# Attention of a fused attention and feed-forward kernel: a fixed table of places for its steps, V's clearing on two engines, the first q on ScalarE's queue

## Chip, cores and metric

One core of one Trainium2 chip. The metric is the device time of one execution in microseconds: 607.05 us for the kernel before, the median of three runs (606.36 to 607.29).

## What is computed

Causal attention over 2 batches, 12 heads, 448 positions and 64 columns a head, then a gated layer (768 to 1536 to 768), then a hard-swish layer (768 to 2048 to 768) on the 896 tokens.

```python
scores = scale * np.matmul(q, k.transpose(0, 1, 3, 2))
scores = np.where(mask, -1000000000.0, scores)
attn = np.exp(scores - max); attn = attn / (sum + 1e-09)
x = np.matmul(attn, v)               # heads side by side: 896 x 768
x = (sigmoid(x @ w_gate) * (x @ w_val)) @ w_out
h = x @ w_in
out = (h * np.clip(h + 3.0, 0.0, 6.0) / 6.0) @ w2_out
```

The weights arrive as 64-bit floats, as their words, and are decoded to 32 bits on the chip.

## The kernel before

Every product is made from three: each operand is split into a high part, rounded to the form that TensorE takes, and a low part, the rest (`TERMS`: high by high, high by low, low by high). Attention works on 12 pairs of heads, pair p = 0 to 11. Six pairs make one batch. After the attention the first feed-forward layer runs in units of a 128-column strip of weights against all tokens, batch 0's half and batch 1's half.

The attention is cut into steps, each a function that issues a few instructions on one engine. The names below are those of the code's keys; a number behind a pair's step is a tile of query rows (0 to 3, of 64, 128, 128 and 128 rows), a tile group of scores or a group of key chunks.

- SP (the queue for loads): **Lq**, **Lk**, **Lv** (`load`, L238 on) and **W** (`load_unit`, L98 on), the raw weights of units 0 to 2.
- TensorE (PE): **T** q and k (`t_pe`, L273), transposes; **S0** to **S2** (`s_pe`), the scores of tiles 0 and 1, of tile 2, of tile 3; **C0** to **C3** (`c_pe`), transposes of the normalised rows; **D0** to **D3** (`d_pe`), products with v; **F** (`f_pe`), the first two units' products for batch 0, 6 steps of 3 products each; **Z** (`z_pe`), idle products on a zero tile, 30 of them.
- ScalarE (ACT): **Th** (`t_hi`), high parts of q and k; **E0** to **E3** (`s_exp`), exponentials and row sums; **H0** to **H3** (`c_hi`) and **X** (`x_hi`), high parts of C and of the output; Wa and Wf of the decoding.
- VectorE (DVE): **Tl** (`t_lo`), low parts; **M0** to **M3** (`s_max`); **R0** to **R3** (`s_rcp`); **J0** to **J3** (`c_lo`); Xl; Wb to We and Wg of the decoding (shift, clamp, join, sign, low part).
- GpSimd (POOL): **V** (`v_hi`, `v_lo`, L262 on), v's two parts into the padded tiles `vpad`; **N0** to **N3** (`s_nrm`), rows times reciprocals.

`rings` says which step must have ended before a buffer is used again. Two PSUM pairs hold scores: S2 of a pair may start when E0 and E1 have read S0's, S0 of the next pair when E2 has read S1's, S1 when E3 has read S2's. One PSUM bank holds the output of D, so D0 waits for Xl of the pair before. C has two banks, so C2 waits for J0 and C3 for J1.

Every engine runs its instructions in the order in which they were issued. That order comes from `emit_in_order(rank)`: a list scheduler. It keeps a modelled clock per engine, takes of all steps whose inputs are done the one that could start first, and breaks ties by `rank`, the pair's number plus a number from the table `LATE` by the step's letter. Steps carry a modelled duration and an engine for this. Ahead of it the code clears the zero halves of `vpad` (three pairs of tiles, two halves each) on VectorE and builds the masks.

Of the kernel before, what the change touches and what calls it, by code (L numbers as in the profile page):

```python
# [31 lines left out]
def kernel(  # L32
# [12 lines left out]
    nc = tc.nc  # L45
    B, H, S, D = q.shape
# [3 lines left out]
    P = 128  # L50
# [7 lines left out]
    NP = B * NPAIR  # L58
# [152 lines left out]
    with tc.manual_schedule():  # L211

        with ExitStack() as actx:
            def pool(name, bufs, **kw):
                return actx.enter_context(tc.tile_pool(name=name, bufs=bufs, **kw))
# [6 lines left out]
            p_sm = pool("p_sm", 8)  # L222
# [203 lines left out]
            def product(cols, stationary=P):  # L426

                return max(cols / 2.4 + 3, stationary / 1.2)


            steps = []
            for p in range(NP):
                def add(key, eng, ns, after, fn, *args):
                    steps.append(((p, key), eng, ns, [(p, a) for a in after], fn, (p, *args)))

                for nm in ("q", "k", "v"):
                    add("L" + nm, "sp", 1500, [], load, nm)
                for nm in ("q", "k"):
                    add("T" + nm, "pe", 390, ["L" + nm], t_pe, nm)
                    add("Th" + nm, "act", 430, ["T" + nm], t_hi, nm)  # L440
                    add("Tl" + nm, "dve", 540, ["Th" + nm], t_lo, nm)
                add("Vh", "pool", 1040, ["Lv"], v_hi)
                add("Vl", "pool", 2150, ["Vh"], v_lo)
                for i, ts in enumerate(STILES):
                    work = sum(
                        6 * product(Q1[t], Q1[t] - Q0[t]) + 2 * product(Q1[t] - Q0[t], 0) for t in ts
                    )
                    add(f"S{i}", "pe", work, ["Tlq", "Tlk"], s_pe, ts)
                    for t in ts:
                        add(f"M{t}", "dve", 70 + 2.1 * Q1[t], [f"S{i}"], s_max, t)  # L450
                for t in range(NQ):
                    n = Q1[t]
                    add(f"E{t}", "act", 605 + 1.67 * n, [f"M{t}"], s_exp, t)
                    add(f"R{t}", "dve", 85, [f"E{t}"], s_rcp, t)
                    add(f"N{t}", "pool", 488 + 1.67 * n, [f"R{t}"], s_nrm, t)
                for g in range(NG):
                    m = WIDTH[g]
                    tiles = [f"N{t}" for t in range(NQ) if Q1[t] > GROUPS[g][0][0] * D]
                    add(f"C{g}", "pe", 0.87 * m, tiles, c_pe, g)
                    add(f"H{g}", "act", 60 + m / 1.2, [f"C{g}"], c_hi, g)  # L460
                    add(f"J{g}", "dve", 70 + m / 0.96, [f"H{g}"], c_lo, g)
                    work = sum(3 * product(S - c * D) for c, _ in GROUPS[g])
                    add(f"D{g}", "pe", work, [f"J{g}", "Vl", f"D{g - 1}"][: 2 + (g > 0)], d_pe, g)
                add("Xh", "act", 430, [f"D{NG - 1}"], x_hi)
                add("Xl", "dve", 540, ["Xh"], x_lo)

            WARM = 30
# [3 lines left out]

            for i in range(WARM):
                steps.append(((0, f"Z{i:02}"), "pe", 300, [], z_pe, (0,)))
# [3 lines left out]
            for u in range(3):  # L477
                w = f"{u}"
                def add(key, eng, ns, after, fn, *args):
                    steps.append(((NP - 3, key + w), eng, ns, after, fn, (u, *args)))  # L480
# [5 lines left out]
                add("Wa", "act", 740, own("W"), dec_scale)  # L486
                add("Wb", "dve", 470, own("W"), dec_shift)
                add("Wc", "dve", 470, own("Wa"), dec_clamp)
                add("Wd", "dve", 870, own("Wb", "Wc"), dec_join)
                add("We", "dve", 870, own("Wd"), dec_sign)  # L490
                add("Wf", "act", 740, own("We"), dec_hi)
                add("Wg", "dve", 870, own("Wf"), dec_lo)
# [6 lines left out]
            for u in range(2):  # L499
                for i in range(KD):  # L500
                    steps.append(
                        ((NP, f"F{u}{i}"), "pe", 570,
                         [(NP - 3, f"Wg{u}"), (NPAIR - 1, "Xl")] + [(NP, f"F{u}{i - 1}")] * (i > 0),
                         f_pe, (u, i))
                    )


            def every(*uses):
                return [((p, a), (p, z)) for p in range(NP) for a, z in uses]
# [9 lines left out]
                (1, [((0, "Tk"), (0, "Tlk"))] + every(("D0", "Xl"))),  # L519
# [3 lines left out]
                (2, every(*((f"S{i}", f"E{ts[-1]}") for i, ts in enumerate(STILES)))  # L523
                    + [((NP, f"F{u}0"), None) for u in range(2)]),
# [3 lines left out]
                (2, [((NP - 3, f"Wa{u}"), (NP - 3, f"Wg{u}")) for u in range(3)]),  # L528
            ]

            HOP = 200

            def emit_in_order(rank):


                left = {s[0]: s for s in steps}
                eng_of = {s[0]: s[1] for s in steps}
                need = {key: set(s[3]) for key, s in left.items()}
                for n, uses in rings:
                    for (a, _), (_, z) in zip(uses[n:], uses):  # L540
                        need[a].add(z)
                    for (a, _), (b, _) in zip(uses[1:], uses):
                        need[a].add(b)
                then = {key: [] for key in left}
                for key, n in need.items():
                    for a in n:
                        then[a].append(key)
                ready = {key: 0 for key, n in need.items() if not n}
                free, done = {}, {}
                while ready:  # L550
                    at, _, key = min(
                        (max(free.get(eng_of[key], 0), t), rank(key), key)
                        for key, t in ready.items()
                    )
                    ready.pop(key)
                    _, eng, ns, _, fn, args = left.pop(key)
                    done[key] = free[eng] = at + ns
                    if eng == "sp":
                        done[key] += 1800
                    fn(*args)  # L560
                    for k in then[key]:
                        if all(a in done for a in need[k]):
                            ready[k] = max(
                                done[a] + HOP * (eng_of[a] != eng_of[k]) for a in need[k]
                            )
                assert not left

            def rank(key):
                p, name = key
                return p + LATE[name[0]]  # L570


            LATE = {
                "J": 1.3, "C": 0.07, "R": -0.94, "E": 0.6, "T": -2.37, "H": 1.3, "S": -0.1,
                "X": 1.38, "M": -2.4, "V": 0.28, "N": 1.41, "D": 2.66, "L": 0.0, "W": 0.85,
                "F": 9.0, "Z": 99.0,
            }


# [15 lines left out]
            emit_in_order(rank)  # L595
# [674 lines left out]
```

## Time and profile before

| What | Value |
|---|---|
| median of three runs | 607.05 us |
| lowest, highest | 606.36, 607.29 us |
| profiled execution: span from first to last instruction | 604.3 us |
| profiled execution: its time beside the span | not given by the page; median less span is 2.75 us |
| TensorE busy | 591.4 us, 98% |
| VectorE, ScalarE, GpSimd busy | 476.4, 346.1, 136.7 us |
| DMA moved | 82.64 MB, mean 137 GB/s |

The attention takes about the first fifth of the span. A busy share of TensorE holds products that wait in its pipeline, so a full share in the attention does not mean that it does useful work all the time; the chain of waits and the starts in the timeline tell that apart. In the timeline an instruction's duration is longer than its distance to the next one where the two overlap, so work is counted by differences of starts.

### The profile page before, as it was taken

What the parts mean: (1) busy time and instruction counts of PE and PEld (TensorE: products, weight loads), DVE (VectorE), ACT (ScalarE), POOL (GpSimd) and SP (SyncE); (2) the same over time, 40 slices, a digit from 0 to 9 for tenths busy, and PEclk for the clock granted to TensorE, in tenths of its full rate; (3) what the DMA queues carried; (4) which work ended last, traced back from release to release, by engine and by line L of the source; (5) the groups of instructions that cost most, each with busy time, mean ns of one, the idle gap of its engine ahead of it and who ended that gap; (6) DMA issues with size and microseconds to landing.
All of it is one profiled execution on the core that took longest, in us unless ns stands there. A gap on an engine that the chain in (4) does not pass through costs nothing.

```text
span 604.3 us, 9071 instructions
## 1 busy us (share of the span) xinstructions
PE 591.4 (98%) x3372; PEld 535.8 (89%) x3372; DVE 476.4 (79%) x739; ACT 346.1 (57%) x680; POOL 136.7 (23%) x195
## 2 busy tenths in 40 slices
PE   8999999999999999999999999999999999999997
PEld 4788788899998999998999999988999899999997
DVE  6789998568797898988967787888999888867601
ACT  3898998735656656667443333387677645533200
POOL 4889988401111111110000000012222000000000
PEclk9999999999999999999999999999999999999999
DMA  7665341036985876674334434367988514437002
GB/s 167 137 178 132 81 143 33 0 79 167 263 178 133 215 183 180 166 177 129 82 114 150 154 115 135 94 165 165 235 217 200 140 53 112 131 124 227 23 1 91
DMA packets 86684, 82.64 MB, mean 137 GB/s; under 512 B 35312, under 2 KB 77040, under 8 KB 86640
## 3 DMA queue, kind: packets, MB, share of 16 engines
q1 hardware_dynamic: 80448, 64.50, 35.9%
q0 software_dynamic: 6192, 17.57, 15.8%
q8 instruction: 26, 0.43, 0.3%
q14 instruction: 18, 0.15, 0.1%
HBM read 61.73 MB, written 2.75 MB: 107 GB/s over the span
## 4 chain that ended last, share of the span: by engine, by line
PE 56%; DVE 27%; ACT 9%; POOL 3%; issue 3%; DMA 2%; SPq 0%; ACTq 0%; POOLq 0%; DVEq 0%
PE w L750 25%; PE m L1203 12%; PE m L190 10%; DVE b L128 4%; DVE b L134 4%; DVE lo L158 4%; PE pav L392 3%; ACT hi L153 3%; PE s L309 2%; DVE g L1171 2%; PE pt L365 2%; DVE b L124 2%; DVE raw L120 2%; ACT pr L337 2%; DVE g L182 2%
## 5 line engine op out<-in xcount | busy, mean ns | idle before, releaser
L1203 PE MATMUL m<-hi,g 128*128 128x384 f32 x448 | 114.0, 335 | 0.6 <-DVE g L1171 0.6
L153 ACT CAST hi<-b 128x768 fp32r<-128x768 f32 x35 | 29.0, 835 | 104.3 <-DVE b L134 100.1
L1203 PEld LDWEIGHTS m<-hi,g 128*128 128x128 f32 x448 | 80.8, 188 | 1.2 <-DVE g L1171 1.2
L1203 PE MATMUL m<-lo,g 128*128 128x384 f32 x224 | 74.9, 335 | 0.4 <-DVE lo L158 0.4
L750 PE MATMUL w<-T,hi 128*128 128x448 f32 x252 | 72.4, 368 | 1.4 <-ACT g2r L767 1.4
L190 PE MATMUL m<-g,hi 128*128 128x448 f32 x288 | 70.1, 365 | 0.0
L134 DVE SCALAR_TENSOR_TENSOR b<-raw,b 128x768 int32<-128x768 int32 x68 | 66.0, 971 | 2.3
L128 DVE SCALAR_TENSOR_TENSOR b<-b,raw 128x768 int32<-128x768 int32 x68 | 65.4, 962 | 2.3
L115 ACT ACTIVATE b<-raw 128x768 f32<-128x768 f32 x68 | 61.2, 905 | 0.0
L124 DVE TENSOR_SCALAR b<-b 128x768 f32<-128x768 f32 x68 | 38.1, 561 | 25.5 <-ACT b L115 25.2
L190 PEld LDWEIGHTS m<-g,hi 128*128 128x128 f32 x288 | 54.1, 188 | 4.3
L144 POOL DMA_DIRECT2D lo<-S x26 | 25.2, 971 | 131.0 <-ACT lo L143 102.5
L352 POOL TENSOR_SCALAR pr<-pr,rc 64x64 f32<-64x64 f32 (+3 forms) x96 | 52.6, 565 | 9.1 <-DVE rc L346 7.3
L158 DVE TENSOR_TENSOR lo<-b,hi 128x768 fp32r<-128x768 f32 x35 | 33.3, 957 | 27.0 <-ACT hi L153 26.9
L750 PEld LDWEIGHTS w<-T,hi 128*128 128x128 f32 x252 | 47.2, 188 | 6.3 <-ACT g2r L767 1.8
L190 PE MATMUL m<-x,hi 128*128 128x448 f32 x192 | 49.1, 367 | 0.0
L337 ACT ACTIVATE pr<-s,nm 64x64 f32<-64x64 f32 (+3 forms) x96 | 44.4, 469 | 5.7 <-PE s L319 5.0
L750 PE MATMUL w<-T,lo 128*128 128x448 f32 x126 | 46.5, 369 | 0.7 <-DMA lo<-S 0.5
L1203 PEld LDWEIGHTS m<-lo,g 128*128 128x128 f32 x224 | 42.0, 188 | 0.7 <-DVE lo L158 0.7
L392 PE MATMUL pav<-pth,vpad 128*128 128x448 f32 (+6 forms) x168 | 41.0, 309 | 0.0
L190 PE MATMUL m<-g,lo 128*128 128x448 f32 x144 | 40.9, 366 | 0.0
L190 PEld LDWEIGHTS m<-x,hi 128*128 128x128 f32 x192 | 35.7, 188 | 2.7
(139 smaller groups left out, 1248.8 us busy)
## 6 DMA issues: line engine op xcount, KB each, us to landing
raw<-in_moe_w_out_dram SPq DMA_DIRECT2D x28, 768.0 KB, 4.5
raw<-in_moe_w_in_dram SPq DMA_DIRECT2D x16, 768.0 KB, 4.7
lo<-S POOLq DMA_DIRECT2D x26, 384.0 KB, 4.3
raw<-in_moe_w_gate_dram SPq DMA_DIRECT2D x12, 768.0 KB, 5.2
raw<-in_moe_w_val_dram SPq DMA_DIRECT2D x12, 768.0 KB, 5.0
k<-in_k_dram SPq DMA_DIRECT2D x24, 112.0 KB, 2.7
q<-in_q_dram SPq DMA_DIRECT2D x24, 112.0 KB, 3.0
v<-in_v_dram SPq DMA_DIRECT2D x24, 112.0 KB, 2.9
```

The costliest lines, as they stand in the source:

```text
L115: nc.scalar.activation(b, words(u)[0].bitcast(F32), AF.Copy, scale=REBIAS)
L124: nc.vector.tensor_scalar(b, b, UPPER_MAX, -UPPER_MAX, op0=ALU.min, op1=ALU.max)
L128: nc.vector.scalar_tensor_tensor(bi, bi, 3, words(u)[1], op0=ALU.logical_shift_left, op1=ALU.bitwise_or)
L134: nc.vector.scalar_tensor_tensor(bi, words(u)[0], -(2 ** 31), bi, op0=ALU.bitwise_and, op1=ALU.bitwise_or)
L153: nc.scalar.copy(hi, part_t[u])
L158: nc.vector.tensor_sub(lo, part_t.pop(u), split_t[u][0].bitcast(F32))
L190: nc.tensor.matmul(ps[:, b, :S], lhsT=w[a][:, i * P : (i + 1) * P], rhs=x(c, k0 + i, b), start=(first and i == 0 and n == 0), stop=(last a ...
L337: nc.scalar.activation(pr[:, :, j], ps[:, j].rearrange("p (c d) -> p c d", d=D), AF.Exp, bias=nm[:, j : j + 1], accum_out=sm[:, j : j + 1],)
L352: nc.gpsimd.tensor_scalar(pr[:, :, j], pr[:, :, j], rc[:, j : j + 1], 1.0, op0=ALU.mult, op1=ALU.mult)
L392: nc.tensor.matmul(live["pav", p][:, c * D :], lhsT=vpad[p % NV][a][:, c], rhs=pt[e][:, off : off + S - c * D], start=(c == 0 and m == 0), ...
L750: nc.tensor.matmul(ps, lhsT=w[a][:, k * P : (k + 1) * P], rhs=x[:, c, i], start=(first and i == 0 and n == 0), stop=(i == HK - 1 and n == ...
L1203: nc.tensor.matmul(po[t], lhsT=g2[2 * s + i][a][:, t * P : (t + 1) * P], rhs=w[e][:, i * HC : (i + 1) * HC], start=(s == 0 and i == 0 and ...
```

## The change

The list scheduler, its modelled engines and durations, `rank` and `LATE` go. Instead `AT` gives each step of a pair a place, the pair adds `p * PERIOD + SHIFT[p]`, and `OWN` gives places to the idle products, the units' decoding and F. A step's place is raised until it lies behind all that it needs, and steps are issued in order of place. The numbers only sort; no instruction waits for one. The number of idle products falls from 30 to 21, the ring of score pairs now names all tiles of a group, p_sm has 16 buffers instead of 8, three of the six tiles of `vpad` are cleared by GpSimd, and pair 0's q is loaded from ScalarE's queue.

```diff
-            p_sm = pool("p_sm", 8)
+            p_sm = pool("p_sm", 16)
...
+                eng = nc.scalar if (p, nm) == (0, "q") else nc.sync
                 for j in range(2):
-                    nc.sync.dma_start(
+                    eng.dma_start(
...
+            PERIOD = 16779
+            SHIFT = [
+                -14386, -7787, -4533, -4454, -1883, 702, 2710, 4993, 6496, 8505, 11307, 14490,
+            ]
+            AT = {
+                "C0": 43560, "C1": 43561, "C2": 51916, "C3": 51917, "D0": 57245, "D1": 57246, "D2": 57247, "D3": 65288,
...
+            OWN = {
...
-            WARM = 30
...
-            for i in range(WARM):
-                steps.append(((0, f"Z{i:02}"), "pe", 300, [], z_pe, (0,)))
+            for i in range(len(WARM)):
+                steps.append(((0, f"Z{i:02}"), [], z_pe, (0,)))
...
-                add("W", "sp", 2000, [], load_unit)
+                add("W", [(2 * u + 2, "Lv")], load_unit)
...
-            def emit_in_order(rank):
+            def emit_in_order():
...
+                def when(key):
+
+                    if key not in place:
+                        p, name = key
+                        at = OWN[name] if name in OWN else p * PERIOD + SHIFT[p] + AT[name]
+                        place[key] = max([at] + [when(a) + 1 for a in need[key]])
+                    return place[key]
+
+                for key in sorted(left, key=lambda key: (when(key), key)):
+                    _, fn, args = left[key]
                     fn(*args)
...
-            for pair in vpad:
-                for t in pair:
+            for i, pair in enumerate(vpad):
+                for x, t in enumerate(pair):
+                    eng = nc.gpsimd if 2 * i + x < 3 else nc.vector
                     for j in range(2):
-                        nc.vector.memset(
+                        eng.memset(
```

What it does to the order is shown at three places. The first is GpSimd's first steps behind the masks, before the change and with it; `vpad_0` and `vpad_1` are the high and low tile of a v, `pr` rows of exponentials.

```order
L264 TENSOR_SCALAR vpad_0_104<-v 64x7x64 x2
L271 TENSOR_TENSOR vpad_1_105<-v,vpad_0_104 64x7x64 x2
L352 TENSOR_SCALAR pr<-pr,rc 64x64 x2
L264 TENSOR_SCALAR vpad_0_106<-v 64x7x64 x2
L271 TENSOR_TENSOR vpad_1_107<-v,vpad_0_106 64x7x64 x2
L352 TENSOR_SCALAR pr<-pr,rc 128x3x64 x2
L352 TENSOR_SCALAR pr<-pr,rc 128x5x64 x2
L352 TENSOR_SCALAR pr<-pr,rc 128x7x64 x2
```

```order
L581 MEMSET vpad_0_104 64x7x64 x2
L581 MEMSET vpad_1_105 64x7x64 x2
L581 MEMSET vpad_0_106 64x7x64 x2
L353 TENSOR_SCALAR pr<-pr,rc 64x64 x2
L353 TENSOR_SCALAR pr<-pr,rc 128x3x64 x2
L353 TENSOR_SCALAR pr<-pr,rc 128x5x64 x2
L353 TENSOR_SCALAR pr<-pr,rc 128x7x64 x2
L265 TENSOR_SCALAR vpad_0_104<-v 64x7x64 x2
```

Three tiles are cleared here, and all four normalisations of pair 0 stand ahead of the first v; before, two v's stood ahead of the second.

The second place is VectorE's first steps behind the masks, again before and then with the change; `kl` and `ql` are the low parts of k and q, `nm` the row maxima.

```order
L592 MEMSET vpad_0_104 64x7x64 x2
L592 MEMSET vpad_1_105 64x7x64 x2
L592 MEMSET vpad_0_106 64x7x64 x2
L592 MEMSET vpad_1_107 64x7x64 x2
L592 MEMSET vpad_0_108 64x7x64 x2
L592 MEMSET vpad_1_109 64x7x64 x2
L293 SCALAR_TENSOR_TENSOR kl<-tr,kh 128x448
L293 SCALAR_TENSOR_TENSOR ql<-tr,qh 128x448
L330 TENSOR_REDUCE nm<-s 64x2
```

```order
L581 MEMSET vpad_1_107 64x7x64 x2
L581 MEMSET vpad_0_108 64x7x64 x2
L581 MEMSET vpad_1_109 64x7x64 x2
L294 SCALAR_TENSOR_TENSOR ql<-tr,qh 128x448
L294 SCALAR_TENSOR_TENSOR kl<-tr,kh 128x448
L331 TENSOR_REDUCE nm<-s 64x2
```

Half of the memsets are gone from ahead of the low parts, and q comes before k.

The third is ScalarE in the middle of the attention, around pair 3's widest exponential (E3, `128x7x64`), before and with the change: `pth` are H, `x00` is X, `qh` and `kh` are Th of pair 5, and the `64x64` row is E0 of pair 4.

```order
L375 CAST pth_758<-pt_730 128x448
L115 ACTIVATE b_770<-raw_657 128x768
L286 ACTIVATE qh_782<-tr_720 128x448
L375 CAST pth_792<-pt_765 128x512
L337 ACTIVATE pr_799,sm_798<-s_744,nm_774 128x7x64 x2
L341 ACTIVATE sm_798<-sm_798 128x2
L405 CAST x00_70<-pav_666 128x448
L375 CAST pth_845<-pt_825 128x512
L375 CAST pth_863<-pt_839 128x320
L286 ACTIVATE kh_866<-tr_847 128x448
L337 ACTIVATE pr_874,sm_873<-s_803,nm_837 64x64 x2
```

```order
L376 CAST pth_731<-pt_721 128x448
L376 CAST pth_733<-pt_726 128x512
L287 ACTIVATE qh_747<-tr_742 128x448
L406 CAST x00_70<-pav_674 128x448
L338 ACTIVATE pr_783,sm_782<-s_703,nm_712 128x7x64 x2
L342 ACTIVATE sm_782<-sm_782 128x2
L376 CAST pth_802<-pt_792 128x512
L376 CAST pth_804<-pt_798 128x320
L287 ACTIVATE kh_818<-tr_813 128x448
L338 ACTIVATE pr_834,sm_833<-s_761,nm_778 64x64 x2
```

X, which needs D3, now stands ahead of E3 and both H's of the first pair of groups ahead of q's cast. With the change this piece comes back with the same kinds of rows in every pair from there on, but for the rows of the decoding.

## Rows read from the trace of the kernel before

**Rows 1.** The windows view; columns: stretch, its length, busy us and instructions (x) of each engine, granted TensorE clock, DMA share, GB/s.
```profile
60.00:100.00 40.00, 38.55 (x339) 32.27 (x340) 37.13 (x76) 36.69 (x126) 37.20 (x54) 1.00 0.36 99
```

**Rows 2.** The chain of waits in order of time: start us, us, what.
```profile
72.75 2.42 POOL pr L352 x2
75.21 0.33 PE pt L365
...
125.17 54.20 PE m L190 x267
```

**Rows 3.** The same chain, one stretch without other engines.
```profile
95.77 0.44 PE tr L277 x4
...
96.75 0.29 PE s L309 x6
...
97.92 0.33 PE pt L365 x3
98.25 0.64 PE s L309 x6
...
99.10 2.29 PE pav L392 x15
101.39 1.12 PE pt L365 x8
...
103.52 0.59 PE pt L365 x5
104.11 0.61 PE pav L392 x6
```

**Rows 4.** The timeline's start: start us, us, engine, line, operation, out<-in, [idle before <-releaser].
```profile
0.74 1.28 ACT L286 ACT_TABLE_LOAD   x1 [0.74 <-PEq L1254]
0.74 0.93 SPq L251 DMA_DIRECT2D k<-in_k_dram  x2
1.19 5.02 PE L470 MATMUL pt<-idle 128*128 128x512 bf16 x12 [1.19 <-DVE idle L582]
1.26 0.21 POOL masks.py:29 MEMSET maskf<- 128x128 f32 x1
2.12 6.63 DVE L592 MEMSET vpad<- 64x448 f32 x12
6.44 1.03 PE L470 MATMUL pt<-idle 128*128 128x512 bf16 x4
8.78 0.63 DVE L293 SCALAR_TENSOR_TENSOR kl<-tr,kh 128x448 fp32r<-128x448 f32 x1
11.15 1.68 DVE L330 TENSOR_REDUCE nm<-s 64x2 f32<-64x128 f32 x3 [1.21 <-PE s L319]
13.80 1.21 POOL L264 TENSOR_SCALAR vpad<-v 64x448 fp32r<-64x448 f32 x2
17.53 3.09 POOL L352 TENSOR_SCALAR pr<-pr,rc 128x192 f32<-128x192 f32 x6
17.80 0.17 DVE L346 RECIPROCAL rc<-sm 128x2 f32<-128x2 f32 x1 [0.84 <-ACT sm L341]
```

**Rows 5.** The page's DMA issues: tensors, queue, count, KB each, median us to landing.
```profile
k<-in_k_dram SPq DMA_DIRECT2D x24, 112.0 KB, 2.7
```

**Rows 6.** The timeline of ScalarE and VectorE in the stretch of rows 3 and before it.
```profile
86.30 0.64 ACT L337 ACTIVATE pr<-s,nm 128x448 f32<-128x448 f32 x1
...
88.64 0.83 ACT L153 CAST hi<-b 128x768 fp32r<-128x768 f32 x1
89.36 0.93 ACT L375 CAST pth<-pt 128x512 fp32r<-128x512 f32 x2
90.15 0.32 ACT L337 ACTIVATE pr<-s,nm 64x64 f32<-64x64 f32 x1
...
91.86 0.94 DVE L158 TENSOR_TENSOR lo<-b,hi 128x768 fp32r<-128x768 f32 x1
92.03 0.51 ACT L337 ACTIVATE pr<-s,nm 128x320 f32<-128x320 f32 x1
```

More of the change, by code (lines that the diff above doesn't have):

```diff
@@ L424 @@
             STILES = [(0, 1), (2,), (3,)]
-            def product(cols, stationary=P):
-                return max(cols / 2.4 + 3, stationary / 1.2)
+            PERIOD = 16779
[3 more added lines that the diff above has]
+            AT = {
[6 rows of a table added]
+            }
+            OWN = {
[6 rows of a table added]
+            }
+            WARM = [
+                -126306, -126306, -126306, -126306, -126306, -126306, -17477.5, -17477.5, -17477.5, -17477.5,
+                -17477.5, 3318.5, 3318.5, 5900.5, 5900.5, 5900.5, 25933.5, 25933.5, 26696.5, 26696.5,
+                26696.5,
+            ]
@@ L431, with add @@
+            OWN.update({f"Z{i:02}": at for i, at in enumerate(WARM)})
             steps = []
             for p in range(NP):
-                def add(key, eng, ns, after, fn, *args):
-                    steps.append(((p, key), eng, ns, [(p, a) for a in after], fn, (p, *args)))
+                def add(key, after, fn, *args):
+                    steps.append(((p, key), [(p, a) for a in after], fn, (p, *args)))
                 for nm in ("q", "k", "v"):
-                    add("L" + nm, "sp", 1500, [], load, nm)
+                    add("L" + nm, [], load, nm)
@@ L444 @@
+                add("Vh", ["Lv"], v_hi)
+                add("Vl", ["Vh"], v_lo)
                 for i, ts in enumerate(STILES):
[L445 to L448, printed above, removed]
+                    add(f"S{i}", ["Tlq", "Tlk"], s_pe, ts)
                     for t in ts:
-                        add(f"M{t}", "dve", 70 + 2.1 * Q1[t], [f"S{i}"], s_max, t)
+                        add(f"M{t}", [f"S{i}"], s_max, t)
@@ L458 @@
                     tiles = [f"N{t}" for t in range(NQ) if Q1[t] > GROUPS[g][0][0] * D]
[L459 to L464, printed above, removed]
@@ L478, with add @@
                 w = f"{u}"
-                def add(key, eng, ns, after, fn, *args):
-                    steps.append(((NP - 3, key + w), eng, ns, after, fn, (u, *args)))
+                def add(key, after, fn, *args):
+                    steps.append(((NP - 3, key + w), after, fn, (u, *args)))
                 def own(*keys):
                     return [(NP - 3, key + w) for key in keys]
-                add("W", "sp", 2000, [], load_unit)
[L486 to L492, printed above, removed]
+                add("W", [(2 * u + 2, "Lv")], load_unit)
+                add("Wa", own("W"), dec_scale)
+                add("Wb", own("W"), dec_shift)
+                add("Wc", own("Wa"), dec_clamp)
+                add("Wd", own("Wb", "Wc"), dec_join)
+                add("We", own("Wd"), dec_sign)
+                add("Wf", own("We"), dec_hi)
+                add("Wg", own("Wf"), dec_lo)
             def f_pe(u, i):
@@ L508, in every @@
             def every(*uses):
-                return [((p, a), (p, z)) for p in range(NP) for a, z in uses]
+                return [((p, a), [(p, x) for x in z]) for p in range(NP) for a, *z in uses]
             last = [
@@ L522 @@
                 (NV, every(("Vh", f"D{NG - 1}"))),
-                (2, every(*((f"S{i}", f"E{ts[-1]}") for i, ts in enumerate(STILES)))
-                    + [((NP, f"F{u}0"), None) for u in range(2)]),
+                (2, every(*((f"S{i}", *(f"E{t}" for t in ts)) for i, ts in enumerate(STILES)))
+                    + [((NP, f"F{u}0"), []) for u in range(2)]),
                 *((2, every((f"E{t}", f"C{last[t]}"))) for t in range(NQ)),
@@ L527 @@
                 (4, every(*((f"H{g}", f"D{g}") for g in range(NG)))),
-                (2, [((NP - 3, f"Wa{u}"), (NP - 3, f"Wg{u}")) for u in range(3)]),
+                (2, [((NP - 3, f"Wa{u}"), [(NP - 3, f"Wg{u}")]) for u in range(3)]),
             ]
-            HOP = 200
-            def emit_in_order(rank):
-                left = {s[0]: s for s in steps}
-                eng_of = {s[0]: s[1] for s in steps}
-                need = {key: set(s[3]) for key, s in left.items()}
+            def emit_in_order():
+                left = {key: (after, fn, args) for key, after, fn, args in steps}
+                need = {key: set(after) for key, (after, _, _) in left.items()}
@@ L539, in emit_in_order @@
                 for n, uses in rings:
                     for (a, _), (_, z) in zip(uses[n:], uses):
-                        need[a].add(z)
+                        need[a].update(z)
                     for (a, _), (b, _) in zip(uses[1:], uses):
                         need[a].add(b)
[L544 to L559, printed above, removed]
-                    fn(*args)
[L561 to L577, printed above, removed]
+                place = {}
+                def when(key):
[4 more added lines that the diff above has]
+                    return place[key]
```

29 lines of the change are left out of this document (15 added, 14 removed), and 11 rows, old and new, of tables (AT, OWN).

## The prediction

> **What bounds the kernel now.** I read the windows view first, for how full each engine is in the attention; then the chain of waits, for which engine ends last; then the timeline of the first 20 us, where the change's two small parts lie. In the window from 60 to 100 us all four engines are busy for 36.7 to 38.6 of 40 us [rows 1]. So no engine can be relieved much, and what an order of steps can win is time in which TensorE waits. The chain shows where that is: up to 75 us it runs through other engines again and again (GpSimd's normalisation last, 2.42 us at 72.75), but from 75.21 us to the end of the attention it is TensorE alone, and so it goes on through 54.20 us of unit products [rows 2]. So the end moves by as much as the end of the attention's TensorE work does, and I count that work.
>
> **TensorE's work.** From a stretch without waits, taking differences of starts [rows 3]: a transpose step T 0.44; S0 1.17, S1 0.85; C0 and C1 together 1.12, S2 then 103.52 - 101.39 - 1.12 = 1.01; C2 0.59, C3 0.33; D0 to D2 2.29, D3 0.61. A pair is 2 x 0.44 + 3.03 + 2.04 + 2.90 = 8.85 us. A product of the unit steps F is 54.20 / 267 = 0.203 [rows 2], and 36 of them are 7.3. The chain tests this: between the starts at 75.54 and 125.17 TensorE does S2 of one pair and S of four (13.1), five T (2.2), C of five and most of a sixth (11.7), D of six and the last half of a seventh (18.9) and 21 F products (4.3), 50.1 by the sum and 49.6 by the clock. So the sum is 1% too high, and I take 1% off.
>
> TensorE's first products for C0 need the normalised rows of all four tiles. When they start, six T, all of S of pair 0 and S0, S1 of pair 1 are done, 7.7 us, both before and after the change. Left are 12 x 8.85 + 7.3 - 7.7 = 105.8, less 1% 104.7 us. Before, GpSimd ends the last normalisation of pair 0 at 17.53 + 3.09 = 20.62 [rows 4]. Without waits F would end at 125.3; it ends at 125.17 + 15 x 0.203 = 128.2. So **2.9 us are lost to waits after C0**, and 20.6 us are the start.
>
> **The start.** *Memsets.* Twelve on VectorE take 6.63 us from 2.12, 0.55 each; the first lo part of k starts only behind them, at 8.78, though its hi part was long done [rows 4]. With six, VectorE is free at 5.4. GpSimd's six cost by the column 448 / 128 x 0.21 = 0.73 each, an estimate from the mask's memset [rows 4], 4.4 in all, and end at about 6.3. GpSimd's next step is the first normalisation, after 10 us, so this is hidden; without that cover it would cost 4.4. *q's load.* It starts beside k's at 0.74 instead of behind its 0.93 us. With 2.7 us to landing [rows 5] and the second half issued half-way, both are there at about 3.9. ScalarE's table load (1.28) stands behind the two issues and is over at 0.74 + 0.93 + 1.28 = 2.95 us, before the data is there. SP issues pair 0's v behind six other loads instead of two, but v is now first used after the normalisation, so nothing waits. *The chain.* Two T end at 4.8, ScalarE's hi parts at about 5.4, VectorE's lo parts follow the memsets, 5.4 + 2 x 0.63 = 6.7, and S0, whose first products start before the second of them is done, ends some 0.9 later, at 7.6. That is the best case, at TensorE's full clock.
>
> The clock is the unknown. Twelve idle products before take 5.02 us, 0.42 each for 512 columns, which is the level of 1.2 GHz; the next four, after some 5 us of unbroken work, take 1.03, near 2.4 GHz [rows 4]. Now six come first, end at about 3.7, and TensorE stands still until q lands. If the low level stays, T takes twice as long, the five idle products ahead of S0 2.1 and S0 2.3: S0 then ends at 5.7 + 2.1 + 2.3 = 10.1. Both ends lie below the 11.15 at which VectorE reads S0 today. I take 8.3, nearer to the fast end, since the gap is short and only the T and idle products fall into it. The Trainium skill, TensorE: Matmul & The Clock Gate, section Part 1: The HAM clock gate, says that the slow clock is the default and that activity releases it; by that rule thinner idle products keep it longer, and the sum would stand nearer to 10.1 and the time some 1.8 us higher. The idle rows agree that it starts slow.
>
> From S0's maximum to the last reciprocal of pair 0 it takes 17.80 - 11.15 = 6.65 us [rows 4], through the same four exponentials with two casts of q and k between; only which cast comes first differs. Today the reciprocal is ready at 17.8, but GpSimd had taken pair 1's v (3.73 us from 13.80) ahead of the normalisations. Now all four normalisations come before any v. Their last one by columns is 448 of 960 of 3.09, 1.4 us. So C0 can start at 8.3 + 6.65 + 0.3 + 1.4 = **16.7** against 20.6: 3.9 us. Pair 0's v then follows, 3.7 us; until D0 needs it TensorE has C0 to C3, S2, S0 and two T, 5.1 us.
>
> **The steady part.** In the table every pair repeats one order. On TensorE: S2(p), C0 and C1(p-1), T of q, D3(p-2), S0(p+1), C2 and C3(p-1), T of k, S1(p+1), D0 to D2(p-1), S2(p+1). Does some other engine take longer than 8.85 a pair? ScalarE is tied in tightest, since its order follows TensorE's: S2 has to wait until E1 has freed its PSUM pair, and E3 stands behind X, which needs D3. Once round: S2 1.01, C0 and C1 1.12, T 0.44, D3 0.61 [rows 3]; E3, X and the cast of k 2.34, H2 and H3 0.79, E0 and E1 1.88 [rows 6]; the sum is **8.19**, so 0.66 of slack. GpSimd has v 3.73 and 3.09 for the three larger tiles [rows 4], with the smallest, under 1, less than 8 us. VectorE's order holds no step that TensorE needs sooner than about 0.6 us after it is ready. So by the rows TensorE sets the pace and no wait is left, and F ends at 16.7 + 104.7 = 121.4 against 128.2, **6.8 us earlier**. Four engines this full will not meet without small waits; a third of today's 2.9 is my allowance, 1.0 us. Forecast: 5.8 us.
>
> **The tail.** Decoding of the first units is spread differently: sign and low part of units 1 and 2 stand at the end of the attention, for unit 2 behind the last X. These are three steps of 0.94 [rows 6], 2.8 us, before unit 3's decode. TensorE has 18 F products, the other halves of units 0 and 1 and all of unit 2 in between, 18 + 36 + 36 at 0.203, 18 us; I cost it at nothing, and 2.8 if VectorE has no slack there. Pair 11's v comes last on GpSimd, 3.73 us, beside C, D3 and three F steps of TensorE, 4 us or more: nothing.
>
> The sum stands against the span of the profiled run, 604.3; the median of the runs is 2.75 above it. I take the difference over: 607.05 - 5.8 = **601.2**.
>
> **Rivals.** *1. The start gives little.* The slow clock stays through S0 (10.1), and waits remain as today: 10.1 + 8.35 + 104.7 + 2.9 = 126.1, so 2.1 us gained, 604.9. For it: the six idle products end before the data. Against: the gap is below 1 us. The Trainium skill, DMA: Bandwidth & Descriptors, section Issuing engines are not separate DMA queues, says that loads issued by different engines share the same DMA engines and only the issuing time is saved; by that the q part alone is worth at most its 0.93 us here, and the forecast takes no more from it.
> *2. ScalarE's round sets the pace, and the kernel is slower.* The table fixes one order, so a late step holds up all behind it, where the old order let the next ready step go first. The round has eight hand-overs between engines. If each costs 0.2 us over the rows, it is 9.8 a pair against 8.85, 1 us lost in each of ten pairs: 121.4 + 10 = 131.4, 3 us later, 610. It decides from 0.15 each, 9.5 a pair. For it: ScalarE's 36.7 of 40 us. Against: the rows' differences of starts hold part of the hand-overs already.
> *3. No change.* Start wins as in rival 1 while the units' decode takes its 2.8 back: 607.
>
> **Chances.** Forecast, 599 to 603: 0.60. Weaker, as rival 1, 603 to 605.8: 0.18. Within 0.2% (1.2 us, about what a measurement of this kernel can tell from no change): 0.08. Slower: 0.14. The range starts at S0 at 7.6 and no waits, 120.7, less half a us for the sum's error, 599.0; upwards it takes in rival 1 and ends at 606.2. The forecast's own range is 599 to 603.
>
> **What would show it.** Right: the lo parts of q and k start before 7 us; C0 of pair 0 at 16 to 18 us; GpSimd has no v before the fourth normalisation; from then on the chain is TensorE alone; the last D ends at about 118.7 (122.4 less 18 F products). Wrong: idle products of 0.42 us after 6 us; ScalarE waiting for D3 and TensorE for E1 in each pair; a distance of S2 to S2 above 9 us; TensorE waiting for a unit's low part between 120 and 140 us.

## Result and profile after

The changed kernel takes 599.95 us, the median of four runs (598.29 to 600.33); the kernel before took 606.7 in four runs beside it. The ratio is 0.9895 with a 95% interval of 0.9871 to 0.9918. Repeated on another occasion the change gave 599.95 again, 0.9891 (0.9871 to 0.9911). The profiled execution took 600.33 us, its span is 598.4.

The page's busy times and its chain by engine, after the change:

```profile
PE 589.3 (98%) x3363; PEld 536.5 (90%) x3363; DVE 473.8 (79%) x733; ACT 345.3 (58%) x680; POOL 136.7 (23%) x201
...
PE 76%; DVE 15%; ACT 5%; issue 2%; DMA 1%; ACTq 0%; DVEq 0%; POOLq 0%
```

The busy shares have hardly moved, which is why they were no help. The windows view of 60 to 100 us, columns as in [rows 1]:

```profile
60.00:100.00 40.00, 40.00 (x352) 34.55 (x351) 33.12 (x73) 36.23 (x127) 33.86 (x57) 1.00 0.30 72
```

TensorE now fills the whole window, the three others have 3.8 to 6.9 us to spare. The chain in order of time shows what that is worth:

```profile
18.93 1.12 PE pt L366 x8
...
79.46 0.81 PE s L310 x6
...
88.18 0.81 PE s L310 x5
...
96.90 0.81 PE s L310 x6
...
117.10 2.86 PE pav L393 x21
119.95 54.80 PE m L190 x270
```

From the first C0 on it is TensorE alone. S2 follows S2 at 88.18 - 79.46 = 8.72 us, the same in the next pair. Where GpSimd and other engines broke the chain up to 75 us [rows 2], nothing does now. The start, which has to be compared with [rows 4]:

```profile
0.73 1.01 ACTq L252 DMA_DIRECT2D q<-in_q_dram  x2
0.73 0.93 SPq L252 DMA_DIRECT2D k<-in_k_dram  x2
1.19 2.74 PE L485 MATMUL pt<-idle 128*128 128x512 bf16 x6 [1.19 <-DVE idle L570]
1.77 2.98 POOL L581 MEMSET vpad<- 64x448 f32 x6
2.12 3.25 DVE L581 MEMSET vpad<- 64x448 f32 x6
5.09 0.98 PE L278 MATMUL tr<-identf,q 112*128 112x112 f32 x4 [1.17 <-DMA q<-in_q_dram]
5.87 0.95 PE L278 MATMUL tr<-identf,k 112*128 112x112 f32 x4
6.61 2.34 PE L485 MATMUL pt<-idle 128*128 128x512 bf16 x5
6.69 0.62 DVE L294 SCALAR_TENSOR_TENSOR ql<-tr,qh 128x448 fp32r<-128x448 f32 x1 [1.33 <-ACT qh L287]
7.43 0.62 DVE L294 SCALAR_TENSOR_TENSOR kl<-tr,kh 128x448 fp32r<-128x448 f32 x1
10.57 0.75 DVE L331 TENSOR_REDUCE nm<-s 64x2 f32<-64x128 f32 x2 [2.51 <-PE s L320]
...
17.52 1.25 POOL L353 TENSOR_SCALAR pr<-pr,rc 128x448 f32<-128x448 f32 x2 [0.70 <-DVE rc L347]
18.74 1.20 POOL L265 TENSOR_SCALAR vpad<-v 64x448 fp32r<-64x448 f32 x2
```

VectorE's lo parts start at 6.69 and 7.43 instead of behind 6.63 us of clearing, and the last normalisation of pair 0 stands ahead of the first v. But S0's maximum is read only at 10.57, against 11.15 before: q landed near 5, and the five idle products after the transposes take 2.34 us for 512 columns each.

For an account I use one more mark, the first product of the layer's w, which TensorE starts when the attention and all unit products for it are through. The timeline rows, of before and then of after:

```profile
179.21 3.81 PE L750 MATMUL w<-x,g 128*128 128x448 f32 x18
```

```profile
174.60 3.81 PE L739 MATMUL w<-x,g 128*128 128x448 f32 x18
```

So **4.6 us** are won up to there. Before, the last normalisation that C0 needs ends at 20.62 [rows 4], and from there to w went 158.6 us; after, C0 to w is 174.60 - 18.86 = 155.7. By this mark the 4.6 are 1.8 of start and 2.9 of waits. The mark is not quite the same on both sides, since before, C0's row starts ahead of that normalisation and is held up inside by 0.3 us:

```profile
19.94 1.50 PE L365 MATMUL pt<-identf,pr 64*128 64x64 f32 x8
```

TensorE's next step, S2, starts at 21.43 before and at 19.97 after; counted from there the 4.6 are 1.5 of start and 3.1 of waits. The other 1.3 us of the span (604.3 - 598.4 is 5.9) lie behind w, in stages that the change does not touch.

### The profile page after: what moved, and what is told of

It reads as the page before. It is cut to its first block, busy times and chain, and to the rows that moved or that the text cites. A ratio compares the mean times of both kernels' runs of the same rounds, so it can differ in the third digit from the quotient of the medians.

```text
span 598.4 us, 9058 instructions
## 1 busy us (share of the span) xinstructions
PE 589.3 (98%) x3363; PEld 536.5 (90%) x3363; DVE 473.8 (79%) x733; ACT 345.3 (58%) x680; POOL 136.7 (23%) x201
## 3 DMA queue, kind: packets, MB, share of 16 engines
HBM read 61.73 MB, written 2.75 MB: 108 GB/s over the span
## 4 chain that ended last, share of the span: by engine, by line
PE 76%; DVE 15%; ACT 5%; issue 2%; DMA 1%; ACTq 0%; DVEq 0%; POOLq 0%
PE m L190 30%; PE w L739 16%; PE m L1192 12%; PE pav L393 6%; PE s L310 4%; PE pt L366 4%; DVE b L128 2%; DVE g L1160 2%; PE tr L278 2%; DVE b L134 2%; PE s L320 2%; DVE b L124 1%; ACT b L115 1%; DVE lo L158 1%; ACT hi L153 1%
## 5 line engine op out<-in xcount | busy, mean ns | idle before, releaser
L353 POOL TENSOR_SCALAR pr<-pr,rc 64x64 f32<-64x64 f32 (+3 forms) x96 | 46.5, 501 | 18.6 <-DVE rc L347 17.2
L393 PE MATMUL pav<-pth,vpad 128*128 128x448 f32 (+6 forms) x168 | 39.0, 306 | 0.0
L331 DVE TENSOR_REDUCE nm<-s 64x2 f32<-64x128 f32 (+3 forms) x48 | 31.7, 678 | 9.1 <-PE s L320 9.0
```

What stands on the lines that cost most here:

```text
L353: nc.gpsimd.tensor_scalar(pr[:, :, j], pr[:, :, j], rc[:, j : j + 1], 1.0, op0=ALU.mult, op1=ALU.mult)
L393: nc.tensor.matmul(live["pav", p][:, c * D :], lhsT=vpad[p % NV][a][:, c], rhs=pt[e][:, off : off + S - c * D], start=(c == 0 and m == 0), ...
```

## Experiments

The table collects, from the timeline of each profiled run, where M0 of pair 0 starts (S0 is over), where C0 of pair 0 starts and where the first w product starts, and the medians. C0 is left empty for the kernels with the old order, whose C0 row starts before its last normalisation has ended (19.94 in before, 19.64 in e2, 20.52 in e12).

| kernel | M0 | C0 | w | C0 to w | w to end | median us (range) | ratio to before, 95% |
|---|---|---|---|---|---|---|---|
| before | 11.15 | | 179.21 | | 425.1 | 606.7 (604.41 to 607.29) | |
| change | 10.57 | 18.86 | 174.60 | 155.7 | 423.8 | 599.95 (598.29 to 600.33) | 0.9895, 0.9871 to 0.9918 |
| e1 | 11.85 | 21.73 | 177.57 | 155.8 | 424.9 | 602.76 (600.82 to 604.65) | 0.9943, 0.9922 to 0.9964 |
| e2 | 10.84 | | 180.35 | | 424.1 | 605.2 (603.43 to 607.96) | 0.9987, 0.9968 to 1.0005 |
| e3 | 8.50 | 16.79 | 172.50 | 155.7 | 424.1 | 598.39 (597.53 to 600.65) | 0.9874, 0.9849 to 0.9899 |
| e4 | 8.91 | 17.20 | 172.92 | 155.7 | 424.5 | 599.04 (597.97 to 600.04) | 0.9881, 0.9859 to 0.9903 |
| e5 | 10.27 | 18.57 | 176.16 | 157.6 | 423.7 | 601.93 (600.43 to 602.38) | 0.9925, 0.9905 to 0.9946 |
| e6 | 10.25 | 18.55 | 190.08 | 171.5 | 423.8 | 614.55 (614.01 to 615.68) | 1.0137, 1.0114 to 1.0159 |
| e7 | 10.68 | 18.98 | 175.84 | 156.9 | 423.9 | 599.59 (599.17 to 601.62) | 0.9897, 0.9875 to 0.992 |
| e8 | 8.19 | 16.48 | 172.22 | 155.7 | 423.4 | 598.17 (597.42 to 599.27) | 0.9868, 0.9846 to 0.989 |
| e9 | 11.20 | 19.50 | 175.22 | 155.7 | 424.3 | 602.18 (601.37 to 603.02) | 0.993, 0.9911 to 0.995 |
| e10 | 10.22 | 18.52 | 174.23 | 155.7 | 423.5 | 599.95 (598.2 to 600.46) | 0.9891, 0.9871 to 0.9911 |
| e11 | 10.74 | 19.04 | 175.84 | 156.8 | 424.9 | 601.32 (601.23 to 602.66) | 0.9918, 0.9898 to 0.9938 |
| e12 | 11.14 | | 181.38 | | 424.8 | 608.02, one run | |

One number runs down the table: with the change's order, C0 to w is 155.7 or 155.8 wherever ScalarE is not loaded and no v stands ahead of GpSimd's normalisations. All that the variants of the start do lies in M0, and in e1 in M0 to C0 too.

**e1, the order alone**: the clearing all on VectorE and q on SP's queue.

```diff
-                eng = nc.scalar if (p, nm) == (0, "q") else nc.sync
+                eng = nc.sync
...
-                    eng = nc.gpsimd if 2 * i + x < 3 else nc.vector
+                    eng = nc.vector
```

> The changed kernel with its two small parts undone: all six tiles of v cleared on VectorE, pair 0's q loaded by SP's queue; the table of places, the 21 idle products and the 16 small buffers stay. If the gain is the order's (waits of 2.9 us after the first C0, normalisations ahead of v), it keeps all but about 1 us: 600 to 601.5 us, ratio to the kernel before 0.990 to 0.992, and TensorE still waits for nothing after the first C0. If the small parts carry the gain, it falls back to 604.5 us or more.

The order alone brings about half of the gain, 0.9943, at 602.76 us, so it lies between the two expectations: 1.3 us above the upper end of the first, and under the second. C0 to w is 155.8: the waits after C0 go without the two small parts. (What is called the order here holds the table, the 21 idle products, the 16 p_sm buffers and the wider ring together; no run takes these apart.) But the start is worse than before's. The waits of TensorE and two windows, columns as above:

```profile
PE s L310 <- DVE kl L294: 2.8, 1, 2.8
```

```profile
8.00:12.00 4.00, 2.02 (x17) 1.72 (x18) 1.92 (x5) 0.00 (x0) 0.00 (x0) 0.64 0.83 185
12.00:16.00 4.00, 3.78 (x18) 2.57 (x19) 2.27 (x6) 2.71 (x12) 0.99 (x3) 0.51 0.59 134
```

With 21 idle products instead of 30 TensorE stands still for 2.8 us until VectorE has cleared, and its granted clock falls to 0.51, the 1.2 GHz level. M0 to C0 takes 9.9 us here and 8.3 in the other runs with this order.

**e2, the two small parts alone**, on the kernel before: three of six tiles cleared by GpSimd, q on ScalarE's queue.

```diff
+                eng = nc.scalar if (p, nm) == (0, "q") else nc.sync
...
-                    nc.sync.dma_start(
+                    eng.dma_start(
...
+                    eng = nc.gpsimd if 2 * i + x < 3 else nc.vector
...
-                        nc.vector.memset(
+                        eng.memset(
```

> The kernel before with the two small parts alone: three of six tiles of v cleared on GpSimd, pair 0's q on ScalarE's queue; list scheduler and 30 idle products as before. If the gain is the order's: 605 to 606.7 us, since the first v of GpSimd and the waits between 20 and 75 us stay. If the small parts carry it: 602 us or less.

No difference that can be measured: the interval holds 1. M0 is 0.3 earlier, but C0 waits for the normalisations behind the v's as before (the first v starts at 5.69 in before and is done long ahead of S0's maximum; it is pair 1's, from 13.80 [rows 4], that holds the normalisations up). So order and clearing need each other: 0.9943 by the order, 0.9987 by the small parts, 0.9895 together.

**e3, the change with q on SP's queue**.

```diff
-                eng = nc.scalar if (p, nm) == (0, "q") else nc.sync
+                eng = nc.sync
```

> The changed kernel with pair 0's q back on SP's queue, ahead of k. In the changed kernel's trace q lands 4.2 us after its issue, since k's load runs beside it, and TensorE stands still from 3.93 to 5.09. Theory: two loads at once share the DMA engines, so q alone lands about 1 us sooner and k no later: T of q starts near 4.0, time 599 to 600 us, no loss. Rival: ScalarE's queue saves q's issue time of about 1 us: 601 us.

```profile
4.21 0.98 PE L278 MATMUL tr<-identf,q 112*128 112x112 f32 x4 [0.28 <-DMA q<-in_q_dram]
5.42 0.58 PE L278 MATMUL tr<-identf,k 112*128 112x112 f32 x4 [0.23 <-DMA k<-in_k_dram]
5.83 1.24 PE L485 MATMUL pt<-idle 128*128 128x512 bf16 x5
8.50 0.75 DVE L331 TENSOR_REDUCE nm<-s 64x2 f32<-64x128 f32 x2 [1.27 <-PE s L320]
```

With the clearing split, loading q beside k is a loss. Behind one another on one queue q lets T start 0.9 us sooner and TensorE's gap is 0.28 instead of 1.17; the five idle products take 1.24 instead of 2.34, and M0 starts 2.1 earlier. By the medians it is 1.6 us (598.39 against 599.95), below the 599 to 600 that were expected; the intervals of the two ratios overlap, so it is the traces that show the loss: T starts at 4.09 to 4.21 in the three profiles with q on SP's queue (e1, e3, e8) and at 4.96 to 5.30 in the eight that have the table and q on ScalarE's. The DMA issues of the first 2 us, of the change and then of e3, give pair 0's q itself:

```profile
q<-in_q_dram ACTq DMA_DIRECT2D x2, 112.0 KB, 3.5
```

```profile
q<-in_q_dram SPq DMA_DIRECT2D x2, 112.0 KB, 2.5
```

**e4, nine idle products ahead of the first T** instead of six, q on ScalarE's queue as in the change.

```diff
             WARM = [
-                -126306, -126306, -126306, -126306, -126306, -126306, -17477.5, -17477.5, -17477.5, -17477.5,
+                -126306, -126306, -126306, -126306, -126306, -126306, -126306, -126306, -126306, -17477.5, -17477.5, -17477.5, -17477.5,
```

> The changed kernel with nine idle products instead of six ahead of the first T, so that TensorE works without a gap until q lands; the rest unchanged. Theory: the gap keeps the 1.2 GHz level until 8.9 us (idle products 0.43 us apart), and this level, by the five idle products ahead of S0, sets S0's start: without the gap the level rises near 6 us, S0 ends at 8.5 to 9 instead of 10.5, time 598 to 598.8 us. Rival: the data and the exponentials set the first C0: 600 us, no change.

```profile
1.19 3.66 PE L485 MATMUL pt<-idle 128*128 128x512 bf16 x9 [1.19 <-DVE idle L570]
...
5.30 0.57 PE L278 MATMUL tr<-identf,q 112*128 112x112 f32 x4 [0.45 <-DMA q<-in_q_dram]
...
6.09 1.24 PE L485 MATMUL pt<-idle 128*128 128x512 bf16 x5
```

q comes no sooner, T starts even 0.2 later, and still M0 is 1.7 earlier: T takes 0.57 for a row that took 0.98, the idle products 1.24 for 2.34, so the gain is TensorE's clock and not the data. M0 at 8.91 stands well clear of the six profiles with the change's start (the change, e5, e6, e7, e10, e11), where it lies at 10.22 to 10.74. By the median the gain is 0.9 us, 599.04 against 599.95, with overlapping intervals; 598 to 598.8 were expected.

**e8, both**: q on SP's queue and seven idle products first.

```diff
-                eng = nc.scalar if (p, nm) == (0, "q") else nc.sync
+                eng = nc.sync
...
-                -126306, -126306, -126306, -126306, -126306, -126306, -17477.5, -17477.5, -17477.5, -17477.5,
+                -126306, -126306, -126306, -126306, -126306, -126306, -126306, -17477.5, -17477.5, -17477.5, -17477.5,
```

> The change with q's first load back on SP's queue and seven idle products instead of six ahead of the first T. Theory (two gains at the same place: q lands some 0.8 us earlier, and TensorE has no gap before T, so its clock is up earlier): C0 at 16.4 to 16.9 us against 18.9 in the change, 597.5 to 598.5 us, at or a little under the run with q on SP's queue alone (598.4). Rival (the one more product delays T and S0 by its 0.43 us instead): 598.8 us.

M0 at 8.19, C0 at 16.48, 598.17 us, the lowest median. It and e3 cannot be told apart by their times, and their intervals overlap the change's a little; in the traces both start C0 some 2 us sooner than the change (1.7 to 2.4 against its two profiles).

**e9, the clearing all on VectorE, q on ScalarE's queue**.

```diff
-                    eng = nc.gpsimd if 2 * i + x < 3 else nc.vector
+                    eng = nc.vector
```

> The change with all twelve clearings of V's buffers back on VectorE, and q still on ScalarE's queue. Theory (VectorE's clearing is what the first Tl waits for once it stands alone, so it hides where q comes from): kl near 9.3 us as in the run with the order alone, TensorE waits there for about 2.8 us and its granted clock falls in the windows 8 to 16 us; 602 to 603.5 us. Rival (q's own late landing adds to it): 603.5 to 604.5 us. Rival (the clearing matters little beside q's queue): 600 to 600.6 us.

```profile
8.78 0.62 DVE L294 SCALAR_TENSOR_TENSOR ql<-tr,qh 128x448 fp32r<-128x448 f32 x1
...
9.32 0.61 DVE L294 SCALAR_TENSOR_TENSOR kl<-tr,kh 128x448 fp32r<-128x448 f32 x1
...
9.99 0.24 PE L310 MATMUL s<-kl,qh 64*64 64x64 f32 x2 [0.90 <-DVE kl L294]
```

kl is at 9.32 as expected, and the time lies in the theory's range, but the reason was half wrong: TensorE waits 0.90 in the profiled run, not 2.8, since with the late q its transposes and idle products end later, and the windows from 8 to 16 us show 1.00. (Four of its six runs had a mean clock of 0.996 or 0.997 and took 602.1 to 603.0, two had 1.000 and 601.4.) With the clearing on one engine q's queue costs nothing (602.18 against 602.76); with the clearing split it costs 1.6 (599.95 against 598.39). Splitting the clearing is worth 4.4 with q on SP's queue and 2.2 with q on ScalarE's (602.18 - 599.95).

**e5 and e6, ScalarE loaded**: X's copy issued twice, and four times, the same source to the same target.

```diff
                 nc.scalar.copy(x_out(p, 0), live["pav", p])
+                nc.scalar.copy(x_out(p, 0), live["pav", p])
```

> X's copy of each pair is issued twice (the same source to the same target), which adds about 0.43 us of ScalarE a pair: its round of 8.19 us becomes 8.62. Theory (TensorE's 8.73 us from S2 to S2 in the profile of the change set the pace, and the 0.66 us of slack that the prediction gave ScalarE is there): nothing moves, 599.4 to 600.6 us. Rival (ScalarE is the bound already, or its handovers have eaten the slack): 0.43 times 11 pairs, 604 to 605 us.

> X's copy of each pair is issued four times: 1.29 us more of ScalarE a pair, 9.48 against TensorE's 8.73. Theory (slack of 0.5 to 0.7 us a pair): ScalarE takes over as the bound and each of some 10 pairs costs 0.75 us more, 606 to 608.5 us, with waits of TensorE for ScalarE's results after C0 in the trace. Rival (the distances of the table hide it: the slack is over 1.3 us): 600 us.

Both were slower than the theory's figure, 601.93 against 599.4 to 600.6 and 614.55 against 606 to 608.5. A copy costs more than I took. ScalarE's timeline in e5, and S2 in the chain of e5, then of e6:

```profile
74.68 0.53 ACT L406 CAST x<-pav 128x448 fp32r<-128x448 f32 x1
75.25 0.53 ACT L407 CAST x<-pav 128x448 fp32r<-128x448 f32 x1
75.67 0.64 ACT L338 ACTIVATE pr<-s,nm 128x448 f32<-128x448 f32 x1
```

```profile
71.48 0.81 PE s L310 x6
...
80.28 0.81 PE s L310 x6
...
89.07 0.81 PE s L310 x6
```

```profile
76.94 0.81 PE s L310 x6
...
86.86 0.81 PE s L310 x6
...
96.78 0.81 PE s L310 x5
```

A copy to the same target starts 0.57 after the first, not 0.43. In e6 S2 follows S2 at 9.92, so ScalarE's round without the three copies is 9.92 - 1.71 = 8.21, hand-overs and all; one copy makes 8.78, and e5 shows 8.80 and 8.79. So ScalarE has **8.72 - 8.21 = 0.5 us of slack** a pair, TensorE sets the pace in the change, and the 0.57 of e5 already tips it. This accounts for most of the loss and not for all of it: 0.08 us in each of eleven pairs would be 0.9 of the 1.9 us by which C0 to w grows in e5, and 1.20 us in each 13.2 of 15.8 in e6. In e5's chain ScalarE and VectorE stand from 90.81 to 104.56, where units are decoded too; the list of waits of e6 has 1.6 us for a unit's low part and 1.1 for a normalisation besides. The rest was not followed pair by pair.

**e7 and e11, pair 0's V between N0 and N1**, its load earlier; e11 is the same once more, beside **e10, the change unaltered**.

```diff
+                        if p == 0 and name in ("Lv", "Vh", "Vl"):
+                            at = SHIFT[0] + AT["N0"] + 0.2
```

> Pair 0's V (1.2 us of GpSimd: Vh and Vl) goes back between N0 and N1, with its load earlier, as the old order had it. Theory (at the start GpSimd's N chain is what the first C0 waits for): C0 starts some 1.2 to 1.6 us later, 601 to 601.8 us in all. Rival (another engine's chain to C0 ends as late, so V there is hidden): 600 us.

> The changed kernel as it is, as a control for the next run and for the later stages: 599 to 600.5 us, with the first unit's w product at 174.4 to 174.8 us. If the 1.4 us wait for g2r near 406 us that before and four of the experiments have, and the first profile of the change has not, is a matter of the kernel, it is absent again; if it is a matter of the run, it can be there.

> Pair 0's V between N0 and N1 once more, beside the control on the same chip. Theory (N is what C0 waits for): the w product 1.2 us later than the control's, and 0.8 to 1.6 us more by the median. Rival: the two medians agree within 0.5 us.

By its median e7 equalled the change of the first occasion and missed the 601 to 601.8 expected (four of its six runs lay at 599.2 to 600.0, two at 601.4 and 601.6). Its trace did not, so it was run again beside the control: 601.32 against 599.95, every run of e11 above every run of e10. The timeline of e11:

```profile
19.04 0.73 PE L366 MATMUL pt<-identf,pr 64*128 64x64 f32 x3
20.67 0.55 PE L366 MATMUL pt<-identf,pr 128*128 128x128 f32 x3 [0.90 <-POOL pr L353]
```

C0's first transposes need only N0 and N1 and start at the same time; the rest waits 0.90 for a later N. C0 to w is 1.1 longer in both profiles. So one v ahead of the normalisations costs about 1.1 us by the traces, 1.4 by e11's median, and nothing by e7's, which stays unexplained. What spread e7's own runs was not seen, since only one was profiled.

**e12, the kernel before, unaltered.**

> The kernel before as it is, for a second profile of it. Theory (in most of its executions TensorE's waits for N let its clock fall for a stretch, which the first profile with its mean clock of 0.999 does not show): a mean clock of 0.993 to 0.997, with a window between 10 and 100 us under 1.00, and 606 to 608 us. Rival (the clock has no part in it): 0.999 or 1.000 in all windows after 10 us.

Its mean granted clock is 0.994, where the first profile of before had 0.999. Windows of e12, and the row of TensorE's wait in it:

```profile
12.00:16.00 4.00, 3.78 (x20) 2.31 (x20) 1.93 (x5) 3.54 (x16) 2.63 (x5) 0.62 0.83 188
60.00:70.00 10.00, 10.00 (x96) 8.27 (x94) 9.79 (x19) 9.53 (x32) 9.66 (x15) 1.00 0.41 94
70.00:80.00 10.00, 8.57 (x57) 7.05 (x55) 8.59 (x18) 7.34 (x24) 7.47 (x10) 0.83 0.21 48
```

```profile
75.80 0.33 PE L365 MATMUL pt<-identf,pr 128*128 128x128 f32 x1 [1.43 <-POOL pr L352]
```

The same wait and the same window in the first profile of before:

```profile
75.21 0.33 PE L365 MATMUL pt<-identf,pr 128*128 128x128 f32 x1 [1.45 <-POOL pr L352]
```

```profile
70.00:80.00 10.00, 8.55 (x76) 7.05 (x75) 9.00 (x19) 8.34 (x28) 8.44 (x12) 1.00 0.21 48
```

The wait is in both; the clock fell in one of them, and there w comes 181.38 - 179.21 = 2.2 later. Seen in windows of 1 us, e12's clock is at 0.50, the 1.2 GHz level, in two stretches, within 11 to 16 us and within 76 to 80 us. The profile of e2, the third one with the old order, has the wait too, and the clock at 0.50 right behind it, within 75 to 79 us, once only; its mean clock is 0.997:

```profile
74.78 0.33 PE L366 MATMUL pt<-identf,pr 128*128 128x128 f32 x1 [1.44 <-POOL pr L353]
```

In the 40 runs of the kernel before that stood beside the three groups of experiments, 11 had a mean clock of 0.999 or 1.000 and a median of 604.84 us, 13 had 0.996 or 0.997 and 606.32, 16 had 0.993 or 0.994 and 607.53. All ten runs of the change had 0.999 or 1.000. So of the 6.75 us between the medians some 4.9 are there at full clock (604.84 - 599.95), and about 1.9 go with the clock that before loses in 29 of 40 runs. That waits like this one set the fall off is the reading nearest to hand, and the change has neither the wait nor the fall; no run took the waits away one at a time, so it is not shown.

## Why the prediction was right, and which steps were not

Direction, size and range held: 601.2 was forecast within 599.0 to 606.2, 599.95 was measured. On the span the sum gave, by the span before, 604.3 - 5.8 = 598.5 and the profile shows 598.4. That closeness is partly luck; taken step by step:

- *TensorE's work after the first C0, 104.7 us.* Right: from C0 at 18.93 to the last D's end at 119.95 and 18 unit products of 54.80 / 270 = 0.203 us is 104.7, and C0 to w is the same within 0.1 in all seven profiles with the table in which ScalarE has no more copies and no v stands ahead of GpSimd's normalisations.
- *2.9 us of waits after C0, which the order removes.* Right, all of them (2.9 or 3.1, by the mark), and without the small parts (e1). The allowance of **1.0 for new small waits** was not needed: in the change's profile TensorE has no listed wait between C0 and w.
- *C0 at 16.7, a gain of 3.9.* **The step that failed**: 18.93, a gain of 1.7. M0 to C0 was right (8.35 forecast, 8.3 measured). S0's end was not: 8.3 taken, 10.57 measured, even beyond the slow bound of 10.1. Two terms were mis-sized. q was to be there at 3.9 and T to start then; T started at 5.09, 1.2 later: the landing time of [rows 5], a median over loads one behind another, was used for two that run side by side. Pair 0's q took 3.5 us from issue to landing in the change, and 2.5 and 2.4 on SP's queue in e3 and e8. And the slow clock was counted for 0.7 of the 2.5 us it could cost; it stayed through T, the idle products and into S0, behind a gap of 1.17 us that was put at under 1. With the clock mended and q as late as in the change (e4) M0 comes at 8.91, with both mended (e8) at 8.19, near the 8.3 forecast; the forecast's best case at full clock, 7.6, was not reached even there. By the Trainium skill, TensorE: Matmul & The Clock Gate, section Part 1: The HAM clock gate, which holds the slow clock to be the default until activity releases it, the start would have been some 1.8 us later than my sum; the trace agrees in direction. It shows 2.3 (10.57 - 8.3), of which e4, with q as late, puts 1.7 on the clock (10.57 - 8.91).
- *q's part is worth at most 0.93 us.* Its sign was wrong: by e3 it is a loss of 2.1 us at w in the trace (1.7 against e10), 1.6 by the medians. The Trainium skill, DMA: Bandwidth & Descriptors, section Issuing engines are not separate DMA queues, allows no more than the issuing time to be saved; the trace agrees: k's issue starts at 0.73 where e3 has it at 1.71, and still T of q and T of k both start later than in e3 (5.09 against 4.21, 5.87 against 5.42).
- *Memsets hidden.* Right; GpSimd's took 0.50 each, not 0.73, and ended at 4.75.
- *ScalarE's round 8.19, slack 0.66.* Right within 0.15: 8.21 by e6, slack 0.5. *Rival 2* was wrong in its premise: the hand-overs are in the differences of starts already. It starts to come true with 0.57 us more on ScalarE (e5). Two sums of the rivals are a little off: eight hand-overs of 0.15 on 8.19 make 9.4 and not 9.5, and the terms of rival 3 give 607.75 and not 607. *Rival 1* had the start (10.1 for S0, 10.57 measured) and not the waits.
- *The tail costs nothing.* Right: 54.80 us of unit products with no break from 119.95 on.
- *The median less the span, 2.75.* Mis-sized: in the change it is about 1.9 (600.33 less 598.4). The first profile of before was an execution with a mean clock of 0.999, which 29 of the 40 runs of that kernel above do not reach. What the change gives back there, some 1.9 us by the runs of before, stood in no term of the forecast; so the span fell by 5.9 where 5.8 was forecast, and the median by 6.75.
- *The signs.* Of those named for right, two did not come: C0 at 16 to 18 us (18.86) and both lo parts before 7 us (6.69 and 7.43); and one of those named for wrong came, idle products of 0.43 us after 6 us. The others held: no v ahead of the fourth normalisation, TensorE alone in the chain, 8.72 us from S2 to S2, and no wait for a unit's low part between 120 and 140 us. The last D ended at 119.95, where 118.7 was named.

So the total came out because a start that was too good by 2.2 stood against an unused allowance of 1.0 and 1.3 us behind w, which the sum did not have. Those 1.3 us are not shown to be the change's. Behind w before shows 425.1 and 424.8 us, the change 423.8 and 423.5, but e7 and e11, the same kernel, differ by 1.0 there. One wait in that part comes and goes, TensorE's for g2r; the lists of waits of the change's first profile and of e10's, the same kernel:

```profile
PE w L739 <- ACT g2r L756: 0.6, 1, 0.6
```

```profile
PE w L739 <- ACT g2r L756: 2.0, 2, 1.4
```

It was in the first profile of before and is missing in e12. So it belongs to the run and not to the kernel; what decides it stays open. Nor does it explain the 1.3 us: the change's profile without it takes 423.8 us behind w, e10's with it 423.5.

## What to carry to other kernels

Where four engines are all over 90% busy, count the work of the one that ends the chain, find from where on it could run without a wait, and forecast that: the constant work came out here to 0.1 us, while the start in front of it was 2.2 us out. Price each part of a change with and without the others: the order wanted the clearing split, the split alone gave nothing, and the third part, q on another queue, was a loss of some 2 us in the traces that the two others hid. Ahead of the first real product, give TensorE idle products until the data lands: here three more of them brought S0's maximum 1.3 to 1.7 us forward in the traces (8.91 against 10.22 and 10.57).

## What was not expected of the hardware

- The same wait of TensorE for GpSimd near 75 us passed at a granted clock of 1.00 in one profile (1.45 us, before) and stood right ahead of a stretch at 0.50 in two (1.44 us in e2, 1.43 us in e12), so it may cost twice; that the wait is the cause is not shown. The 18 runs of before in e1's group spread over 3.8 us (604.26 to 608.08), the ten of the change, which has no such wait, over 2.3 (598.2 to 600.46).
- The granted clock in the windows view reads 1.00 from 4 to 8 us in the change's profile, while its idle products stand 0.43 us apart there, 1.2 GHz; at the start of this program the starts of equal products tell the level, the column does not.
- Pair 0's q landed 3.5 and 3.3 us after its issue when k's load ran beside it from another queue (the change, e10), and 2.4 to 2.5 us after it when k followed on the same queue (e1, e3, e8).
